# Masking half the units on ScalarE and GpSimd, a one-step leaky rectifier, 32-bit weight rests and a new static order

## The chip, the cores and the metric

The program runs on one core of a Trainium2 chip. The metric is device time in microseconds (us) from launch to the end of one execution. Engines: PE is the matrix engine (PEld its weight loads), DVE the vector engine, ACT the scalar engine, POOL the GpSimd engine, and SP the queue that issues the transfers (DMA).

## The reference

Attention with a top-32 mask on 4 batches of 8 heads, 576 positions and 64 dimensions, then two feed-forward layers on the 2304 tokens:

```
scores = q @ k^T / 8
kth    = the 32nd largest score of each row
scores = where(scores >= kth, scores, -1e9)
attn   = exp(scores - max); attn = attn / (sum(attn) + 1e-9)
x      = attn @ v, heads side by side               # 2304 x 512
h = x @ w1_in;  g = max(0.01 * h, h);               x = g @ w1_out    # 512 -> 2048 -> 512
h = x @ w2_in;  g = s * max(h, 0)^2 + b;          out = g @ w2_out
```

The weights arrive as float64 bits; nothing is converted on the host.

## The kernel before, in words

All products are made in float16 halves: a number is scaled by a power of two and split into a high and a low float16, and a product takes three matrix products (high x high, high x low, low x high).

**Units and tiles.** The 2304 tokens make 18 tiles of 128 rows (two of the 18 are made of the last 64 rows of two batches). A unit is one tile and one pair of heads, so there are 72 units, four to a tile. A unit runs: `qk` on PE (scores into PSUM), `s_ev` on ACT (copy to the tile `s`), on DVE for each head four rounds of `max` (the eight largest, `mx`) with three `match_replace` (`wk`) between them, which leave the 32nd largest score in the last place of `mx`; `expo` on ACT (`em`); `mask` on DVE, which multiplies the exponentials by (score >= 32nd) and sums them (`L811`); then the halves `e_hi` on ACT and `e_lo` on POOL, a transposing transfer `e_turn` into `ahl`, `pv_mm` on PE, and `x_ev` on DVE (`L904`), which writes the unit's columns of the tile's row block `x`. The first `EB` units (7) make their halves and the transpose on PE instead of `e_lo` and `e_turn`.

**Weights.** Each of the four matrices (1i, 1o, 2i, 2o) has 16 blocks of 512 KB. A block is loaded (`w_load`), DVE moves exponent and fraction into place (`w_shift`, `L343`), ACT rounds the rest of the fraction (`w_rest`, `L348`), DVE keeps sign and top exponent bit (`w_sign`, `L353`), POOL adds the two as integers (`w_round`, `L357`). Four blocks share a scale, from a norm that PE makes (`w_norm`). The halves are then made in one of the ways that `WM` names: P by PE and ACT, D with a DVE step (`lo_d`, `L454`), G with a DVE step (`pre`) and a POOL step. 1i and 1o stay on the chip; the halves of 2i and 2o go to memory (`w_out`). `finals1` (`L541`) ends the preparation of layer one, `finals` (`L558` to `L570`) that of layer two.

**Feed-forward.** Tiles are taken in blocks, one tile at a time for the first ten and two at a time for the other eight. Each layer: `m_in` (`L1022`, 12 products for each of 16 weight blocks, 128 or 256 columns), the rectifier in groups of 128x512 (`a1` to `a5`), `m_out` (`L1093`, 3 products of 512 columns for each tile and weight block). In layer one the leaky rectifier is `a1` = relu on ACT, `a2` = a second, negated and scaled relu on ACT (`L1054`), `a3` = their difference on POOL (`L1058`). The weights of layer two are streamed from memory for each block of tiles by 512 KB loads (`st_i`, `st_o`); two of the 16 pairs stay on the chip.

**The order.** A planner (`Plan`) writes the order of every engine's instructions before the program is built: each engine takes, when it is free in the plan, the ready step with the lowest key. Keys come from `W0`, `WD` (weights), `KO` (offsets of loads and first units) and the unit's number; the durations in the `add` calls, `HOP` (from one engine to the next) and the buffers of each ring (`BUFS`) decide when a step is ready. On the chip each engine then runs its list in that order and waits where an operand isn't there. The rings `em` and `ahl` have one buffer, `s` has four, `raw` three.

## Time and profile before

| what | us |
|---|---|
| three executions | 1250.7, 1255.13, 1255.96 (median 1255.13) |
| the profiled execution, first to last instruction (span) | 1250.3 |
| busy: PE / DVE / ACT / POOL | 1070.3 / 1036.9 / 827.4 / 842.1 |
| layer one's scales ready (`L541`) | 186.15 |
| 12th, 13th and 72nd `x_ev` | 310.17, 320.11, 1098.27 |
| last PE instruction to the end | 1246 to 1250.3 |

The profile gives no device time of its own for the profiled execution; its span lies 0.4 us under the fastest of the three. Busy time of PE is modelled at its ends: successive products overlap by a little, so the starts in the timeline are the better measure of what a group costs (start to start). On DVE a `max` shows 0.744 us but the next instruction starts 0.66 us after it.

### The profile page before, as it was taken

What the parts mean: (1) busy time and instruction counts of PE and PEld (TensorE: products, weight loads), DVE (VectorE), ACT (ScalarE), POOL (GpSimd) and SP (SyncE); (2) the same over time, 40 slices, a digit from 0 to 9 for tenths busy, and PEclk for the clock granted to TensorE, in tenths of its full rate; (3) what the DMA queues carried; (4) which work ended last, traced back from release to release, by engine and by line L of the source; (5) the groups of instructions that cost most, each with busy time, mean ns of one, the idle gap of its engine ahead of it and who ended that gap; (6) DMA issues with size and microseconds to landing.
All of it is one profiled execution on the core that took longest, in us unless ns stands there. A gap on an engine that the chain in (4) does not pass through costs nothing.

```text
span 1250.3 us, 27997 instructions
## 1 busy us (share of the span) xinstructions
PE 1070.3 (86%) x10520; PEld 735.6 (59%) x10520; DVE 1036.9 (83%) x2437; ACT 827.4 (66%) x1427; POOL 842.1 (67%) x1126
## 2 busy tenths in 40 slices
PE   2666767788888988988998989789989799899998
PEld 1333334556666766665776666566566466666665
DVE  4999899999989999999999999889999999800000
ACT  7887998866577766667876665558876565444321
POOL 5776555657678877677887776658887666655542
PEclk9877898999999999999999999989999999999999
DMA  7767776478889898888899797988445568510444
GB/s 180 237 217 213 198 199 198 148 165 211 218 158 240 199 263 183 220 201 223 221 237 248 165 249 162 261 231 195 83 80 114 149 162 228 153 26 18 133 162 161
DMA packets 362408, 228.39 MB, mean 183 GB/s; under 512 B 276512, under 2 KB 301088, under 8 KB 362272
## 3 DMA queue, kind: packets, MB, share of 16 engines
q1 hardware_dynamic: 362272, 226.61, 71.5%
q8 instruction: 82, 1.34, 0.5%
q14 instruction: 54, 0.44, 0.1%
HBM read 151.52 MB, written 13.11 MB: 132 GB/s over the span
## 4 chain that ended last, share of the span: by engine, by line
DVE 24%; PE 22%; DMA 17%; POOL 9%; issue 4%; ACT 4%; SPq 1%; DVEq 0%; POOLq 0%; ACTq 0%
DMA ahl<-ehl 10%; DVE mx L786 9%; PE acc L1093 9%; PE h L1022 9%; DVE wk L795 8%; DVE em L811 5%; POOL ehl L869 3%; DMA st_o<-sc_2o 2%; PE pv L897 2%; POOL g L1070 2%; DMA qn<-in_q_dram 1%; POOL r L1058 1%; PE sc L768 1%; DMA vn<-in_v_dram 1%; DMA st_i<-sc_2i 1%
## 5 line engine op out<-in xcount | busy, mean ns | idle before, releaser
L786 DVE MAX8 mx<-wk 128x8 f32<-128x576 f32 x432 | 311.3, 744 | 0.0
L1093 PEld LDWEIGHTS <-g 128*128 128x128 f16 x1728 | 159.5, 98 | 141.0 <-issue 23.7
L1022 PE MATMUL h<-early,wreg 128*128 128x128 f16 (+1 forms) x2688 | 224.2, 235 | 5.1 <-DMA early<-xhl 3.5
L1022 PEld LDWEIGHTS <-wreg 128*128 128x128 f16 x2688 | 194.3, 98 | 52.8 <-issue 5.1
L1093 PE MATMUL acc<-wreg,g 128*128 128x512 f16 x864 | 222.8, 380 | 0.2 <-DVE o L1152 0.2
L795 DVE MATCH_REPLACE8 wk<-mx,wk 128x576 f32<-128x576 f32 x288 | 212.7, 741 | 0.0
L1093 PE MATMUL acc<-st_o,g 128*128 128x512 f16 x756 | 194.5, 379 | 12.9 <-DMA st_o<-sc_2o 12.6
L869 POOL TENSOR_TENSOR ehl<-em,ehl 128x576 f16<-128x576 f32 x130 | 168.0, 1298 | 50.1 <-ACT ehl L865 49.7
L1022 PE MATMUL h<-xT,st_i 128*128 128x128 f16 (+1 forms) x2352 | 198.5, 236 | 2.3 <-DMA st_i<-sc_2i 2.0
L1022 PEld LDWEIGHTS <-st_i 128*128 128x128 f16 x2352 | 170.3, 99 | 45.5 <-DMA st_i<-sc_2i 5.0
L1050 ACT ACTIVATE r<-h,cg 128x512 f32<-128x512 f32 x144 | 98.3, 683 | 93.7 <-PE h L1022 74.8
L811 DVE SCALAR_TENSOR_TENSOR em<-s,mx,em 128x576 f32<-128x576 f32 x144 | 155.0, 1087 | 0.3 <-ACT em L808 0.2
L865 ACT CAST ehl<-em 128x576 f16<-128x576 f32 x130 | 86.4, 668 | 93.0 <-DVE em L811 67.1
L808 ACT ACTIVATE em<-s,st,est 128x576 f32<-128x576 f32 x144 | 121.8, 861 | 18.9 <-POOL st L789 14.9
L1067 ACT ACTIVATE g<-r 128x512 f16<-128x512 f32 x144 | 89.9, 626 | 64.1 <-PE acc L1093 44.5
L897 PE MATMUL pv<-vhl,ahl 128*128 128x64 f16 (+3 forms) x2160 | 86.6, 201 | 49.8 <-DMA ahl<-ehl 47.6
L897 PEld LDWEIGHTS <-ahl 128*128 128x128 f16 (+1 forms) x2160 | 79.6, 104 | 71.9 <-DMA ahl<-ehl 66.8
L1058 POOL TENSOR_TENSOR r<-r,early 128x512 f32<-128x512 f32 x72 | 93.6, 1300 | 38.2 <-ACT early L1054 37.9
L1062 POOL TENSOR_TENSOR early<-r 128x512 f32<-128x512 f32 x72 | 75.7, 1052 | 62.1 <-ACT r L1050 61.4
L774 ACT COPY s<-sc 128x576 f32<-128x576 f32 x144 | 91.5, 636 | 35.0 <-PE sc L768 31.8
L768 PE MATMUL sc<-kT,qT 128*128 128x288 f16 (+1 forms) x640 | 99.2, 297 | 11.2 <-ACT s L774 9.7
L786 DVE MAX8 mx<-s 128x8 f32<-128x576 f32 x144 | 107.0, 746 | 0.3 <-ACT s L774 0.3
(191 smaller groups left out, 1741.0 us busy)
## 6 DMA issues: line engine op xcount, KB each, us to landing
st_i<-sc_2i SPq DMA_DIRECT2D x98, 512.0 KB, 4.8
st_o<-sc_2o SPq DMA_DIRECT2D x98, 512.0 KB, 4.8
raw_2i<-in_moe_w_in_dram SPq DMA_DIRECT2D x16, 512.0 KB, 4.9
wreg<-in_moe_w_in_dram SPq DMA_DIRECT2D x16, 512.0 KB, 5.7
raw_1o<-in_moe_w_out_dram SPq DMA_DIRECT2D x16, 512.0 KB, 4.0
raw_2o<-in_moe_w_out_dram SPq DMA_DIRECT2D x16, 512.0 KB, 4.1
qn<-in_q_dram SPq DMA_DIRECT2D x16, 256.0 KB, 4.8
sc_2i<-hl_2i SPq DMA_DIRECT2D x16, 256.0 KB, 2.4
```

What stands on the lines that cost most here:

```text
L768: nc.tensor.matmul(pt[a, c, 0:288], lhsT=qT[u][:, h, z, a], rhs=kT[b, p][:, 576 * h + 288 * c:576 * h + 288 * c + 288], start=(z == 0), st ...
L774: nc.scalar.copy(sc[u, h], box["pt"][:, :, 0:288])
L786: nc.vector.max(out=mx[u][:, h, r, :], in_=wk[u, h] if r else flat(sc[u, h]))
L795: nc.vector.match_replace(out=wk[u, h], in_to_replace=mx[u][:, h, r, :], in_values=src, imm_value=NEG)
L808: nc.scalar.activation(em[u][:, h, :], flat(sc[u, h]), AF.Exp, bias=st[u][:, h:h + 1], scale=est[:, 0, u:u + 1])
L811: nc.vector.scalar_tensor_tensor(em[u][:, h, :], flat(sc[u, h]), mx[u][:, h, 3, 7:8], em[u][:, h, :], op0=ALU.is_ge, op1=ALU.mult, accum_o ...
L869: nc.gpsimd.tensor_tensor(ehl[u][:, 1, a], em[u][:, h, :], ehl[u][:, 0, a], op=ALU.subtract)
L897: nc.tensor.matmul(pt[a, o0:o1], lhsT=ahl[u][:, za, blk * P + a.start:blk * P + a.stop], rhs=vt[:, zv, v0:v1], start=(i == 0 and za == 0 a ...
L1022: nc.tensor.matmul(box["h"][:, n * T:(n + 1) * T], lhsT=w[:, ew, c, :], rhs=src[:, ex, c, :], start=(c == 0 and ew == 0 and ex == 0), stop ...
L1050: nc.scalar.activation(box["r1"], box["h"], AF.Relu, scale=cg[:, 2 * l, 3, gi:gi + 1])
L1058: nc.gpsimd.tensor_tensor(box["r1"], box["r1"], box["r2"], op=ALU.subtract)
L1093: nc.tensor.matmul(accs[i, l, tt], lhsT=ghl[i, l, g][:, eg, n * T + tt * P:n * T + (tt + 1) * P], rhs=w[:, ew], start=(f == 0 and eg == 0 ...
```

## The change

- **The mask of three units in eight** (`MK`, letters A; 27 of 72 units): POOL multiplies the 32nd largest score by 2^98 (`t_big`); ACT writes relu(2^98 x 32nd - 2^98 x score), which is zero where the score is kept and huge where it isn't (`above`); POOL subtracts that from the score (`less`); ACT takes the exponential and sums it (`expo2`). The DVE mask falls away there. The other 45 units are as before.
- **The leaky rectifier** of layer one is one ACT step (`AF.Prelu`, slope 0.01); `a2` and the POOL difference are gone.
- **The rest of the weights** is written as a 32-bit integer; `w_sign` reads the raw word and the shifted word, keeps the upper two bits of the first and joins them (two tensors, 32 bits, instead of one, 16 bits), and no longer waits for `w_rest`.
- **Smaller ones:** P-made weight halves 56 instead of 48 blocks, `lo_d` and `pre` 4 each instead of 8; norms of four blocks in one go; ten instead of seven units turned by PE; `raw` two buffers instead of three.
- **The order** is written with other durations, a model of transfers by kind (`XFER`), steps of DVE and POOL that hold each other up in the plan (`lock`), rings that are taken in the order of the code (`IN_LINE`), other keys, the matrices in the order 1i, 1o, 2o, 2i, and all 18 tiles one at a time (`BLOCKS`).

```diff
-BUFS = {... "raw": 3, ...}
-WM = {"1i": "PPP", "1o": "P", "2i": "PG", "2o": "DP"}
-ORDER = ("1i", "1o", "2i", "2o")
+BUFS = {... "raw": 2, ...}
+WM = {"1i": "PPPP", "1o": "PPPP", "2i": "GPPP", "2o": "PPDP"}
+ORDER = ("1i", "1o", "2o", "2i")
+IN_LINE = ("mx", "em", "ehl", "ahl", "x32", "s", "wk", "kT", "vT", "qT", ...)
+MK = "DADDAADD"
-EB = 7
+EB = 10
-W0 = {"1i": -14.81, "1o": -9.79, "2i": -14.83, "2o": -0.65}
+W0 = {"1i": -39.03, "1o": -3.45, "2i": -32.04, "2o": -4.3}
-NB = 10
+BLOCKS = [1, 1, 1, 1, 1, 1, 1, 1, 1, 1, 1, 1, 1, 1, 1, 1, 1, 1]
...
         def w_rest(m=m, f=f):
-            nc.scalar.activation(t[:, :, 0], t[:, :, 1], AF.Copy, scale=2.0 ** -13)
+            nc.scalar.activation(raw[m, f].rearrange("p (n t) -> p n t", t=2)[:, :, 0], t[:, :, 1], AF.Copy, scale=2.0 ** -13)
         def w_sign(m=m, f=f):
-            nc.vector.tensor_scalar(t[:, :, 1], t[:, :, 3], 0xC000, None, op0=ALU.bitwise_and)
+            d = wT[m, f].bitcast(I32)
+            nc.vector.scalar_tensor_tensor(d, raw[m, f].rearrange("p (n t) -> p n t", t=2)[:, :, 1], -(1 << 30), d,
+                                           op0=ALU.bitwise_and, op1=ALU.bitwise_or)
...
+            def t_big(u=u):
+                nc.gpsimd.tensor_tensor(st[u][:, 8:10], mx[u][:, :, 3, 7], big.to_broadcast([P, 2]), op=ALU.mult)
+            def above(u=u, h=h):
+                nc.scalar.activation(em[u][:, h, :], flat(sc[u, h]), AF.Relu, bias=st[u][:, 8 + h:9 + h], scale=-BIG)
+            def less(u=u, h=h):
+                nc.gpsimd.tensor_tensor(em[u][:, h, :], flat(sc[u, h]), em[u][:, h, :], op=ALU.subtract)
+            def expo2(u=u, h=h):
+                nc.scalar.activation(em[u][:, h, :], em[u][:, h, :], AF.Exp, bias=st[u][:, h:h + 1], scale=est[:, 0, u:u + 1],
+                                     accum_out=st[u][:, 2 + h:3 + h])
+            if MK[u % len(MK)] == "D":
...
+            else:
+                if h == 0:
+                    x_big = add(POOL, 0.15, t_big, mxd, key + 0.7, use=[tm])
+                x = add(ACT, 0.6, above, [x_big] + ([x_exp] if h else []), ...)
+                x = add(POOL, 1.37, less, [x], ...)
+                mk.append(add(ACT, 0.8, expo2, [x, ex[h]], ...))
...
             def a1(g=g, box=box):
-                nc.scalar.activation(box["r1"], box["h"], AF.Relu, scale=cg[:, 2 * l, 3, gi:gi + 1])
-            def a2(g=g, box=box):
-                nc.scalar.activation(box["r2"], box["h"], AF.Relu, scale=cg[:, 1, 3, g * nf // 4:g * nf // 4 + 1])
                 if l == 0:
-                    nc.gpsimd.tensor_tensor(box["r1"], box["r1"], box["r2"], op=ALU.subtract)
+                    nc.scalar.activation(box["r1"], box["h"], AF.Prelu, scale=cg[:, 0, 3, gi:gi + 1], alpha=0.01)
```

What the planner makes of it is seen in the lists of the engines. First DVE, where it comes to layer one's scales (`finals1`; `cg` are the scales, `mx` and `wk` the rounds of a unit, `T_2o` and `raw_2o` a weight block). Before, from row 305 of 1847:

```order
L353 TENSOR_SCALAR raw_2o_1648<-raw_2o_1648 128x512
L303 TENSOR_SCALAR cg<-cg 128x1
L343 TENSOR_SCALAR T_2o_1725<-raw_2o_1663 128x512
L413 TENSOR_SCALAR cI_1o_1729<-ident,cg 128x128
L534 TENSOR_REDUCE consts<-cg 128x1
L541 SCALAR_TENSOR_TENSOR cg<-cg 128x4
```

After, from row 197 of 1777:

```order
L371 TENSOR_SCALAR T_2o_1273<-raw_2o_1230 128x512
L331 TENSOR_SCALAR cg<-cg 128x1
L829 MATCH_REPLACE wk_1_1228<-mx_1151,wk_1_1228 128x576
L381 SCALAR_TENSOR_TENSOR T_2o_1273<-raw_2o_1230,T_2o_1273 128x512
L442 TENSOR_SCALAR cI_1o_1280<-ident,cg 128x128
L569 TENSOR_REDUCE consts<-cg 128x1
L576 SCALAR_TENSOR_TENSOR cg<-cg 128x4
```

Ahead of `finals1` stood 49 `max`, 10 masks, 50 shifts and 49 sign steps; now 28 `max`, 4 masks, 34 shifts and 34 sign steps. At the 12th `x_ev` there stood 104 `max`, 25 masks, 8 `lo_d`, 8 `pre`; now 106, 16, 4 and 4.

Second PE, behind the last attention product (`h` is what `m_in` writes, `acc` what `m_out` writes). Before, the last rows of it and the first of each kind behind it:

```order
L897 MATMUL pv_16270<-vhl_94,ahl_16233 128x64
L1093 LDWEIGHTS g_0_1_16168
L1093 MATMUL acc_0_1_16206<-wreg,g_0_1_16168 128x512
L1022 LDWEIGHTS wreg
L1022 MATMUL h_0_6_16251<-early,wreg 128x256
```

After:

```order
L956 MATMUL pv_17932<-vhl_96,ahl_17876 128x64
L1081 LDWEIGHTS wreg
L1081 MATMUL h_0_2_17881<-early,wreg 128x128
L1151 LDWEIGHTS g_0_1_17822
L1151 MATMUL acc_0_0_17809<-wreg,g_0_1_17822 128x512
```

Behind the last attention product stood 51 `m_in` steps of 256 columns (19 of layer one, 32 of layer two) and 123 `m_out` steps; now 69 `m_in` steps of 128 columns (21 and 48) and 73 `m_out` steps. Between the 12th and the end of the 72nd attention product stood 272 `m_in` steps of 128 and 77 of 256 columns, 413 `m_out` and 130 `qk` steps; now 459 of 128 columns, 463 `m_out` and 129 `qk`.

Third ACT, where it masks an A unit now (`em` is the unit's tile, `ahl` and `etp` another unit's halves). After:

```order
L903 CAST ahl_2821<-etp_8_2848 128x128
L855 ACTIVATE em_2851<-s_0_2619,st_2650 128x576
L910 CAST ahl_2821<-etp_8_2848 128x128
L855 ACTIVATE em_2851<-s_1_2696,st_2650 128x576
L861 ACTIVATE em_2851,st_2650<-em_2851,st_2650,est 128x576
L808 COPY s_0_2881<-sc_0_2871 128x576
```

The two `above` steps stand close together ahead of the first exponential, which waits for POOL's first `less`; the next unit's score copy stands behind it. ACT's list holds one table load before and one now.

## Rows read from the trace of the kernel before

**Rows 1.** Page, parts 1 and 2: busy us of each engine, busy tenths.

```profile
PE 1070.3 (86%) x10520; PEld 735.6 (59%) x10520; DVE 1036.9 (83%) x2437; ACT 827.4 (66%) x1427; POOL 842.1 (67%) x1126
DVE  4999899999989999999999999889999999800000
```

**Rows 2.** Windows: stretch, its us, busy us (instructions) per engine, clock, DMA share, GB/s.

```profile
0.00:186.00 186.00, 113.69 (x575) 60.23 (x575) 161.20 (x373) 158.32 (x252) 117.18 (x158) 0.88 0.74 208
186.00:310.00 124.00, 102.34 (x1082) 69.75 (x1080) 121.47 (x283) 94.45 (x161) 79.12 (x96) 0.96 0.68 175
310.00:798.00 488.00, 436.06 (x5346) 319.70 (x5342) 464.66 (x1109) 336.56 (x604) 365.90 (x520) 0.99 0.89 214
310.00:1098.00 788.00, 706.88 (x7887) 509.82 (x7884) 745.68 (x1752) 524.06 (x931) 577.41 (x812) 0.99 0.80 194
1098.00:1250.00 152.00, 147.34 (x989) 95.83 (x985) 8.58 (x31) 50.61 (x86) 68.36 (x60) 1.00 0.32 99
```

**Rows 3.** Timeline, DVE: start, us; scales ready, 12th, 13th, 49th, 72nd `x_ev`.

```profile
186.15 0.16 DVE L541 SCALAR_TENSOR_TENSOR cg<-cg 128x4 f32<-128x4 f32 x1
310.17 0.28 DVE L904 TENSOR_TENSOR x<-pv,st 128x128 f32<-128x128 f32 x1
320.11 0.28 DVE L904 TENSOR_TENSOR x<-pv,st 128x128 f32<-128x128 f32 x1
799.28 0.29 DVE L904 TENSOR_TENSOR x<-pv,st 128x128 f32<-128x128 f32 x1 [2.77 <-PE pv L897]
1098.27 0.29 DVE L904 TENSOR_TENSOR x<-pv,st 128x128 f32<-128x128 f32 x1 [8.18 <-PE pv L897]
```

**Rows 4.** Timeline, PE: start to start gives what each kind of step costs.

```profile
605.02 0.65 PE L768 MATMUL sc<-kT,qT 128*128 128x288 f16 x4
605.51 0.83 PE L1022 MATMUL h<-xT,st_i 128*128 128x128 f16 x12
606.18 0.81 PE L1093 MATMUL acc<-kept_o,g 128*128 128x512 f16 x3
...
1097.20 1.03 PE L897 MATMUL pv<-vhl,ahl 128*128 128x128 f16 x27
1098.07 0.81 PE L1093 MATMUL acc<-wreg,g 128*128 128x512 f16 x3
1098.72 1.47 PE L1022 MATMUL h<-early,wreg 128*128 128x256 f16 x12
1100.03 0.81 PE L1093 MATMUL acc<-wreg,g 128*128 128x512 f16 x3
```

**Rows 5.** Groups by line: busy us, mean ns of one, idle us before it.

```profile
L811 DVE SCALAR_TENSOR_TENSOR em<-s,mx,em 128x576 f32<-128x576 f32 x144 | 155.0, 1087 | 0.3 <-ACT em L808 0.2
L353 DVE TENSOR_SCALAR raw_1o<-raw_1o 128x512 uint16<-128x512 uint16 x16 | 14.2, 891 | 3.1 <-ACT raw_1o L348 2.9
L454 DVE SCALAR_TENSOR_TENSOR hl_2o<-T_2o,cg,hl_2o 128x512 f16<-128x512 f32 x8 | 9.0, 1129 | 0.0
L448 DVE TENSOR_SCALAR T_2i<-T_2i,cg 128x512 f32<-128x512 f32 x8 | 5.6, 724 | 0.0
L348 ACT ACTIVATE raw_1o<-raw_1o 128x512 uint16<-128x512 uint16 x16 | 21.9, 1390 | 0.0
L1054 ACT ACTIVATE early<-h,cg 128x512 f32<-128x512 f32 x72 | 49.2, 683 | 1.1 <-POOL g L1070 1.1
L808 ACT ACTIVATE em<-s,st,est 128x576 f32<-128x576 f32 x144 | 121.8, 861 | 18.9 <-POOL st L789 14.9 <-POOL ehl L869 3.7
L1058 POOL TENSOR_TENSOR r<-r,early 128x512 f32<-128x512 f32 x72 | 93.6, 1300 | 38.2 <-ACT early L1054 37.9 <-POOL vhl L666 0.2
```

**Rows 6.** Two DVE lines with two inputs: ns of one, min/median/max.

```profile
L811 DVE SCALAR_TENSOR_TENSOR em<-s,mx,em x144: 775/873/1901, 35.1 to 1086.7; 128x576 f32<-128x576 f32 x144
L454 DVE SCALAR_TENSOR_TENSOR hl_2o<-T_2o,cg,hl_2o x8: 719/914/1812, 200.3 to 249.0; 128x512 f16<-128x512 f32 x8
```

**Rows 7.** DMA view, 310 to 798 us: all that was moved.

```profile
DMA packets 182481, 104.41 MB, mean 214 GB/s; under 512 B 147591, under 2 KB 151687, under 8 KB 182414
```

More of the change, by code (lines that the diff above doesn't have):

```diff
@@ L99, in order @@
         remain = [t[1] for t in self.by_tok]
+        line = {r: iter(self.rings[r].line) for r in IN_LINE}
+        turn = {r: next(line[r], None) for r in IN_LINE}
         last = [0.0] * len(remain)
         start, self.end, moved = [None] * N, [0.0] * N, 0.0
-        events = []
+        events, held = [], {"DVE": 0.0, "POOL": 0.0}
         for n in range(N):
@@ L134, in order @@
                     for k in self.take[n]:
-                        self.rings[self.by_tok[k][0]].live.append(k)
+                        r = self.rings[self.by_tok[k][0]]
+                        r.live.append(k)
+                        if self.by_tok[k][0] in turn:
+                            turn[self.by_tok[k][0]] = next(line[self.by_tok[k][0]], None)
+                            for e_, it in r.wait:
+                                heapq.heappush(events, (now, it[1], "ready"))
+                            r.wait = []
                     start[n] = now
@@ L269 @@
     nc.vector.memset(neg1, -1.0)
+    big = one.tile([P, 1], F32, name="big")
+    nc.vector.memset(big, BIG)
     tiny = one.tile([P, 2], F32, name="tiny")
@@ L881 @@
                 lo.append((x, y))
[L882 removed]
+            x = add(SP, XFER["e_turn"], e_turn, [y for _, y in lo], ke, take=[ta], use=[th])
             lo = [(x, x)]
@@ L918 @@
     blocks, t = [], 0
-    for n in [1] * NB + [2] * ((NTL - NB) // 2):
+    for n in BLOCKS:
         blocks.append(list(range(t, t + n)))
@@ L1075, in layer @@
                 x = add(ACT, 0.571, a1, [x, fin1], ka, take=[t1], use=[th])
-                x = add(ACT, 0.571, a2, [x], ka, take=[t2], use=[th])
-                x = y = add(POOL, 1.225, a3, [x], ka, use=[t1, t2])
                 x = add(ACT, 0.52, a4, [x], ka, take=[tg], use=[t1])
```

202 lines of the change are left out of this document (113 added, 89 removed).

## Prediction

> **What bounds the kernel now.** I read the page first, then the same engines by stage, then the places where the stages meet. The page shows two engines that are both nearly full, PE at 86% and DVE at 83% of the span [rows 1]. But the row of tenths shows that DVE is at nine almost everywhere up to slice 35 and at zero behind it: DVE sets the pace of the first 1098 us, PE alone that of the last 152 [rows 1, 3]. The windows make three stages of it [rows 2]. In the first, up to 186 us, the weights are prepared: DVE is busy for 161 and ACT for 158 of 186 us, PE for only 114, since layer one cannot start before its scales are there (186.15 us, rows 3). From the 12th `x_ev` (310 us) to the 72nd (1098 us) DVE is busy for 745.7 of 788 us, which is 94.6%, PE for 707, POOL for 577, ACT for 524. Behind that PE is busy for 147 of 152 us and DVE for 9.
>
> So there are three clocks to follow: when the early work is done, how fast a unit goes by in the middle, and how much of the feed-forward work is left for PE behind the last unit.
>
> **Prices.** On PE start to start is the price [rows 4]: `qk` 0.49 us, `m_in` of 128 columns 0.67, of 256 columns 1.31, `m_out` 0.65, `pv_mm` 0.87. A tile taken alone therefore costs PE as much as in a pair (2 x 0.67 against 1.31); what it costs more is DMA, since each block of tiles streams layer two's weights again.
>
> **The early stage.** DVE is the engine to count. Up to the 12th `x_ev` nine masks go (25 to 16, 1.087 us each, -9.8), four `lo_d` (1.129, -4.5) and four `pre` (0.724, -2.9), and two `max` and one `match_replace` come (about +2) [rows 5]. The sign step is new: two tensors of 32 bits in place of one of 16, 64 times. No row shows it; the nearest is `lo_d`, also two 128x512 tensors in and one out, with 0.719 us at best, 0.914 in the middle and 1.129 in the mean, against 0.891 of the old step [rows 5, 6]. The bounds are 64 x (0.719 - 0.891) = -11 us and 64 x (1.129 - 0.891) = +15; I take the middle value, +1.5. Sum: -14, say 15 us, because the sign step also stops waiting for `w_rest` (the 3.1 us of the one matrix shown). The 13th `x_ev` moves from 320 to 305 us. The scales of layer one move further: 21 `max`, 6 masks, 16 shifts and 15 sign steps that stood ahead of them now stand behind, so PE gets feed-forward work some 45 to 55 us earlier. I give that no term of its own; it only means that PE is not behind when the middle begins.
>
> The mask shows 775 ns at best and 1901 at worst, `lo_d` 719 and 1812 [rows 6]. The Trainium skill (GPSIMD Engine Reference, Specifications) says that GpSimd shares its SBUF interfaces with the vector engine, against instructions with two SBUF inputs among others; the spread of both lines agrees with that. By that rule the new sign step, with its two inputs, is as exposed as `lo_d`, which would put it at the mean and the early sum at 15 - 13.7 = about 1 us instead of 15.
>
> `w_rest` costs ACT 1.390 us now; with 32-bit output it lies between that and 0.683, the price of a 512-element ACT step with 32-bit output [rows 5]. That is 0 to 45 us of ACT, which is not the engine I count, so it is worth nothing by itself; if it stays at 1.39, ACT at 158 of 186 us is no worse off than before, as 16 blocks less stand ahead of the scales.
>
> **The middle.** DVE: from the 12th to the 72nd `x_ev` 119 masks become 74, 45 x 1.087 = -49 us, so its 745.7 us become 697 [rows 2, 5]. ACT: `above` and the exponential's sum come in 23 units, 46 steps of about 0.86 at most (+40, priced by the exponential), and 60 `a2` of 0.683 go (-41): nothing. POOL: 46 `less` at 1.300 come (+60), 60 differences at 1.300 go (-78): about -18 of 577 [rows 2, 5]. Neither becomes a bound. What A units do add is a longer way from the last `max` to the halves: `t_big`, `above`, `less`, `expo2` across two engines, about 0.2 + 0.7 + 1.3 + 0.9 = 3.1 us and four hand-overs in place of one mask of 1.1. Behind `above` on ACT stand the next unit's score copy and the rectifier; behind `less` on POOL the next unit's small steps; the single `em` and `ahl` buffers mean that the next unit's exponential waits for them.
>
> PE: the change of `BLOCKS` and of the keys puts feed-forward work into this stage that stood behind it. From behind the 12th to the end of the 72nd attention product, before: 272 x 0.67 + 77 x 1.31 + 413 x 0.65 + 130 x 0.49 + 60 x 0.87 = 667 us. After: 459 x 0.67 + 463 x 0.65 + 129 x 0.49 + 60 x 0.87 = 724 us [rows 4]. It was 667 of the 778 us from the 13th to the 72nd `x_ev`; now PE has 724, more than DVE's 697, and becomes the engine that sets the pace.
>
> DMA: from 310 to 798 us, where tiles go one by one, its engines are busy for 0.89 of the time, 434 us for the 37 units between the 12th and the 49th `x_ev`, 11.7 us and 104.4/37 = 2.82 MB for a unit [rows 2, 3, 7]. All units now go like that. For 59 units this is 692 us.
>
> So 724 (PE), 697 (DVE) and 692 (DMA) lie within 5% of each other. None can be filled wholly, because each engine runs a fixed list and waits for the others. Before, the engine that bound filled 94.6%. I take the same for PE: 724/0.946 = 765 us in place of 778.
>
> **The end.** Behind the last attention product stood 51 x 1.31 + 123 x 0.65 = 147 us of PE work; the trace shows 152 us from the last `x_ev` to the end [rows 2, 3, 4], so some 5 us for waits and the last store. Now it is 69 x 0.67 + 73 x 0.65 = 94 us. Layer two of three tiles lies in these 94 us, one alone at the end, with fewer other steps to fill a wait; I add 8 us: 102, which is 50 us less.
>
> **The sum.** 305 + 765 + 102 = 1172 us of span, against 320 + 778 + 152 = 1250. The profiled execution is given by its span alone, 1250.3, which is 4.8 us under the median of the three runs (and 0.4 under the fastest); I add these 4.8: **1177 us**, 6% less than 1255.13.
>
> **Rivals.**
>
> *PE runs through (0.14).* At the end of the kernel PE fills 147 of about 148 us when nothing holds it. If the new order feeds it as well in the middle, that takes 730 us: 305 + 730 + 102 + 4.8 = 1142. For it: layer one starts earlier, so there is always feed-forward work at hand. Against it: PE, DVE and DMA are too close together.
>
> *The middle gains nothing (0.19).* The longer way of the A units with one `em` buffer eats what DVE gave up, or the early stage stays where it is. Then the middle takes 778 us (1190) or up to 13.8 us for a unit, 815 us (1227). For it: PE's waits for `ahl` and DVE's 8 us wait ahead of the last `x_ev` [rows 3] show that the attention chain is already late at times. Still faster, since the end is shorter in any case.
>
> *DMA binds, and it gets slower (0.08).* 59 units of 2.82 MB are 166 MB. From 310 to 1098 us the queues moved 194 GB/s in the mean [rows 2]; if that were all that a full middle gets, it would take 858 us, and 305 + 858 + 102 + 4.8 = 1270. It decides from below 198 GB/s, where the middle passes 843 us. For it: share 0.89 already, most packets under 512 B [rows 7]. Against: 214 GB/s at that share, which leaves 240 at a full one. The Trainium skill (DMA: Bandwidth & Descriptors, Specifications) gives about 358 GB/s as the limit of one core's memory; by that there would be no such case. The trace doesn't agree that this is the limit that counts here, as 0.89 is reached at 214.
>
> **How the numbers follow.** 0.59 for the forecast, whose own range is 1151 to 1199 (PE filled to 98% or 92% in the middle: 739 or 787 us), 0.14, 0.19 and 0.08 for the rivals. The range from 1143 to 1222 takes in nearly all of the first two and most of the third. About 0.5%, 6 us, is what can be told from no change. All but the DMA case are faster; it splits into 0.06 slower and 0.02 about equal, and I leave 0.01 of the others for about equal and 0.01 for slower: faster 0.90, same 0.03, slower 0.07.
>
> **What would show it.** Right: 90 masks on DVE; layer one's scales before 140 us; the 13th `x_ev` near 305; about 12.9 us for a unit behind that; PE busy near 95% in the middle, and about 100 us from the last `x_ev` to the end. The sign step near 0.9 us, `w_rest` nearer 0.7. Wrong: DMA share near 1 with waits for `st_i` and `st_o` over 30 us on PE (the DMA case); DVE idle for more than 80 us in the middle with waits on ACT's exponential or POOL's `less` (the chain); or scales still at 186 us.

## The result, and the profile after

The changed kernel takes 1268.97 us (median of 4 runs, 1266.42 to 1274.95) against 1252.91 us before, timed beside it on the same chip: a ratio of 1.0129, 95% interval [1.0095, 1.0164]. It is slower by 1.3%, where 1177 us and 6% less had been forecast. The profiled span is 1268.7 us where the sum said 1172, so 97 us are to be found.

The page of the changed kernel, parts 1 and 2, answers to [rows 1]: busy us of each engine, then busy tenths of DVE.

```profile
PE 1092.3 (86%) x12116; PEld 771.0 (61%) x12116; DVE 970.7 (77%) x2321; ACT 801.5 (63%) x1483; POOL 803.6 (63%) x1125
DVE  4649888897999679898887898888669999993100
```

DVE gave up 66 us, as meant, but it no longer has a nine in nearly every slice: it waits, in the early stage and in the middle. The windows of the changed kernel, cut where the forecast cut them (13th and 72nd `x_ev`), answer to [rows 2]; columns as there.

```profile
0.00:354.50 354.50, 246.64 (x1809) 150.01 (x1810) 278.53 (x671) 241.83 (x470) 201.61 (x270) 0.85 0.64 184
354.50:1166.00 811.50, 750.85 (x9266) 553.62 (x9264) 684.82 (x1633) 531.03 (x966) 565.33 (x822) 0.99 0.86 208
1166.00:1268.70 102.70, 94.82 (x1047) 67.39 (x1044) 7.31 (x18) 28.68 (x48) 36.62 (x33) 1.00 0.67 214
```

Stage by stage, forecast against measured: early 305 and 354.5 (+49.5), middle 765 and 811.5 (+46.5), end 102 and 102.7 (+0.7). The end is right; the two losses are nearly equal in size and, as the runs below show for most of them, different in kind.

The groups by line of the changed kernel answer to [rows 5]: mask, sign step (two of its four groups), rest, and the two new steps of an A unit.

```profile
L845 DVE SCALAR_TENSOR_TENSOR em<-s,mx,em 128x576 f32<-128x576 f32 x90 | 83.6, 940 | 7.8 <-ACT em L842 7.8
L381 DVE SCALAR_TENSOR_TENSOR T_1o<-raw_1o,T_1o 128x512 int32<-128x512 int32 x16 | 12.5, 797 | 0.0
L381 DVE SCALAR_TENSOR_TENSOR T_2o<-raw_2o,T_2o 128x512 int32<-128x512 int32 x16 | 11.2, 698 | 0.0
L376 ACT ACTIVATE raw_1o<-raw_1o 128x512 int32<-128x512 uint16 x16 | 10.9, 684 | 3.3 <-DMA raw_1o<-in_moe_w_out_dram 3.2
L855 ACT ACTIVATE em<-s,st 128x576 f32<-128x576 f32 x54 | 40.4, 769 | 22.7 <-POOL st L849 22.4
L858 POOL TENSOR_TENSOR em<-s,em 128x576 f32<-128x576 f32 x54 | 77.2, 1443 | 16.0 <-ACT em L855 13.2 <-PE sc L802 2.8
```

The prices were not the fault. The sign step came out below the forecast (0.70 to 0.80 us for 0.91), the rest at its lower end (0.68), `above` below (0.77 for 0.86); only `less` is dearer (1.44 for 1.30).

**The middle, by who waits for whom.** Four groups of the changed kernel, 354.5 to 1166 us; the number behind the bar's second half is the idle time before them and what ended it.

```profile
L1151 PE MATMUL acc<-st_o,g 128*128 128x512 f16 x588 | 159.6, 382 | 12.3 <-DMA st_o<-sc_2o 11.0 <-ACT vj L676 1.2
L956 PE MATMUL pv<-vhl,ahl 128*128 128x64 f16 (+2 forms) x1809 | 69.8, 198 | 38.7 <-DMA ahl<-ehl 38.3 <-DVE wk L829 0.2
L963 DVE TENSOR_TENSOR x<-pv,st 128x128 f32<-128x128 f32 x59 | 16.9, 287 | 59.4 <-PE pv L956 59.0
L820 DVE MAX8 mx<-s 128x8 f32<-128x576 f32 x114 | 85.6, 750 | 17.5 <-ACT s L808 17.5
```

PE waits for the turned exponentials (`ahl`, a transfer) and for streamed weights. DVE waits most for PE's attention product (59.0 us), and for 17.5 us for ACT's copies of the scores. DVE idles for 127 of 811 us, which the prediction had named as the sign of the A units' chain, but the releasers are mostly others: for an exponential of ACT it waits 6.3 us, for POOL's denominators 15.6 us, and 13.5 us of these last remain in the run below that has every mask on DVE. The queue that issues all transfers, SP, waits too (what it waited for: us in total, times, longest); L1060 loads layer two's weights for the stream.

```profile
SPq L1060 <- PE h L1081: 93.5, 49, 9.8
SPq L1060 <- PE acc L1151: 61.4, 36, 4.1
```

Such a load waits until PE has done with the buffer that it will fill, and every turn of exponentials behind it in the queue waits with it. The two lines make 155 us; in the middle of the kernel before they were 75.5 and 47.7, 123 us. At the turns themselves SP waits still longer, for POOL's halves: 196 us over all of POOL's steps. But that was 214 us before, so it is not what the change added.

**The early stage.** SP's timeline of the kernel before, then of the changed one (start, us): first turns and loads of weights.

```profile
10.27 1.35 SPq L738 DMA_TRANSPOSE qT<-qhl  x1
11.67 0.57 SPq L334 DMA_DIRECT2D raw_2i<-in_moe_w_in_dram  x1
12.47 1.31 SPq L617 DMA_TRANSPOSE kT<-khl  x1
```

```profile
2.14 3.68 SPq L362 DMA_DIRECT2D wreg<-in_moe_w_in_dram  x4
...
17.79 1.35 SPq L772 DMA_TRANSPOSE qT<-qhl  x1
...
23.72 4.15 SPq L651 DMA_TRANSPOSE kT<-khl  x1
```

The new keys put four loads of weights ahead of the first unit's keys, and ten ahead of the first turn of keys (`kT`), where one stood before. The first unit's scores come later, and its first `max` later still. ACT's copy of these scores and that `max`, before and then after:

```profile
19.91 0.62 ACT L774 COPY s<-sc 128x576 f32<-128x576 f32 x1
20.76 0.75 DVE L786 MAX8 mx<-s 128x8 f32<-128x576 f32 x1
```

```profile
35.05 0.66 ACT L808 COPY s<-sc 128x576 f32<-128x576 f32 x1
50.26 0.74 DVE L820 MAX8 mx<-s 128x8 f32<-128x576 f32 x1
```

Before, the `max` starts 0.2 us after its scores are there; now it starts 14.5 us after, behind shifts and sign steps of weights that stand ahead of it in DVE's list. The first `x_ev` starts at 106 us (51 before). Windows of the first 100 us, before and then after, show what DVE does meanwhile (its busy time is the third, behind PE's and PEld's).

```profile
0.00:50.00 50.00, 19.55 (x107) 12.74 (x107) 31.98 (x82) 40.01 (x74) 30.24 (x55) 1.00 0.78 205
50.00:100.00 50.00, 34.03 (x158) 17.34 (x159) 46.95 (x101) 39.93 (x56) 35.88 (x39) 0.76 0.74 229
```

```profile
0.00:50.00 50.00, 15.66 (x54) 8.48 (x55) 25.66 (x58) 33.25 (x68) 33.45 (x49) 0.87 0.95 272
50.00:100.00 50.00, 34.54 (x131) 17.91 (x130) 28.84 (x84) 32.12 (x63) 31.16 (x48) 0.69 0.42 110
```

DVE works for 54.5 of 100 us where it worked for 78.9. First the transfers are full (0.95), and then they are more than half idle (0.42). Up to the first `x_ev` DVE idles for 46 us (18 before), from there to the 13th for 30 (10 before): 48 us more in all, which is the loss of this stage. Of the 46 us it waits 11.0 for loads of weights, 8.8 for ACT's sums of squares of the queries, 8.6 for PE's norms of the keys, and the rest in small parts for further steps of other engines. PE's granted clock is 0.85 of full speed in the mean of this stage (0.91 before); what that costs no run tells.

### The profile page after: what moved, and what is told of

Its sections match the earlier page's. It is cut to its first block, busy times and chain, and to the rows that moved or that the text cites. A ratio compares the mean times of both kernels' runs of the same rounds, so it can differ in the third digit from the quotient of the medians.

```text
span 1268.7 us, 31192 instructions
## 1 busy us (share of the span) xinstructions
PE 1092.3 (86%) x12116; PEld 771.0 (61%) x12116; DVE 970.7 (77%) x2321; ACT 801.5 (63%) x1483; POOL 803.6 (63%) x1125
## 4 chain that ended last, share of the span: by engine, by line
PE 42%; DMA 32%; DVE 9%; ACT 7%; POOL 4%; issue 3%; SPq 2%; POOLq 0%; ACTq 0%; DVEq 0%
PE h L1081 16%; DMA ahl<-ehl 16%; PE acc L1151 15%; DMA st_o<-sc_2o 4%; PE pv L956 4%; DVE mx L820 3%; PE sc L802 3%; DMA st_i<-sc_2i 3%; DMA qT<-qhl 2%; DVE wk L829 2%; DMA qn<-in_q_dram 2%; DMA raw_2i<-in_moe_w_in_dram 1%; PE wlo_1i L491 1%; POOL ehl L928 1%; DMA wreg<-in_moe_w_in_dram 1%
## 5 line engine op out<-in xcount | busy, mean ns | idle before, releaser
L1081 PEld LDWEIGHTS <-wreg 128*128 128x128 f16 x3456 | 215.4, 99 | 54.0 <-issue 3.2
L1081 PE MATMUL h<-early,wreg 128*128 128x128 f16 x3456 | 236.6, 220 | 0.7 <-DMA early<-xhl 0.5
L1151 PE MATMUL acc<-wreg,g 128*128 128x512 f16 x864 | 235.5, 382 | 0.0
L1081 PEld LDWEIGHTS <-st_i 128*128 128x128 f16 x3024 | 183.4, 98 | 42.8 <-DMA st_i<-sc_2i 7.6
L1081 PE MATMUL h<-xT,st_i 128*128 128x128 f16 x3024 | 200.9, 219 | 5.5 <-DMA st_i<-sc_2i 5.5
L928 POOL TENSOR_TENSOR ehl<-em,ehl 128x576 f16<-128x576 f32 x124 | 157.7, 1283 | 50.8 <-ACT ehl L924 49.0
L1129 POOL TENSOR_TENSOR g<-r,g 128x512 f16<-128x512 f32 x72 | 84.6, 1175 | 76.3 <-ACT g L1126 76.0
L820 DVE MAX8 mx<-s 128x8 f32<-128x576 f32 x144 | 107.9, 750 | 17.5 <-ACT s L808 17.5
L829 DVE MATCH_REPLACE8 wk<-mx,s 128x576 f32<-128x576 f32 x144 | 106.8, 742 | 0.0
L1113 ACT ACTIVATE r<-h,cg 128x512 f32<-128x512 f32 x72 | 49.3, 684 | 69.5 <-PE h L1081 69.1
L845 DVE SCALAR_TENSOR_TENSOR em<-s,mx,em 128x576 f32<-128x576 f32 x90 | 83.6, 940 | 7.8 <-ACT em L842 7.8
```

The source lines that it names most:

```text
L820: nc.vector.max(out=mx[u][:, h, r, :], in_=wk[u, h] if r else flat(sc[u, h]))
L829: nc.vector.match_replace(out=wk[u, h], in_to_replace=mx[u][:, h, r, :], in_values=src, imm_value=NEG)
L845: nc.vector.scalar_tensor_tensor(em[u][:, h, :], flat(sc[u, h]), mx[u][:, h, 3, 7:8], em[u][:, h, :], op0=ALU.is_ge, op1=ALU.mult, accum_o ...
L928: nc.gpsimd.tensor_tensor(ehl[u][:, 1, a], em[u][:, h, :], ehl[u][:, 0, a], op=ALU.subtract)
L1081: nc.tensor.matmul(box["h"][:, n * T:(n + 1) * T], lhsT=w[:, ew, c, :], rhs=src[:, ex, c, :], start=(c == 0 and ew == 0 and ex == 0), stop ...
L1129: nc.gpsimd.tensor_tensor(ghl[i, l, g][:, 1], box["v"], ghl[i, l, g][:, 0], op=ALU.subtract)
```

## The experiments

Fifteen further kernels were run. Letters of theories belong to the expectation that they stand in. "New order" is the changed kernel's, "old order" that of the kernel before; a kernel "in its own order" has the same instructions in the same places, with more buffers or less data. The three stages are given as early + middle + end, from one profiled execution each.

**A third buffer for the weights' bits.** The change cut these from three to two. The first run gives the buffer back without planning anew, the second plans with it.

```diff
+REAL = {"raw": 3}
-        return pl.tile(shape, dtype, tag=name, name=label, bufs=BUFS[name])
+        return pl.tile(shape, dtype, tag=name, name=label, bufs=REAL.get(name, BUFS[name]))
```

> The changed kernel with its order of instructions unchanged, but a third buffer for the raw weight blocks (the plan still counts two). Theory A, the early stage is held by the two raw buffers (48 blocks come in between 57 and 269 us, about 4.0 us each for 2o and 2i, though load, rest, shift, sign and round of one block follow each other in about 7.8 us): loads are issued earlier, the blocks of 2o and 2i come every 3 us or less, layer two's scales come before 280 us instead of 297, and the time falls by 10 to 20 us. Rival, the static lists of DVE, ACT and POOL hold the pace and the loads only fit them: scales within 5 us of 297, time within 5 us of 1269.

> The changed kernel with three raw buffers in the plan too, so the order is written anew with the same keys. Theory A: layer two's scales near 260 us, 13th x_ev near 320 instead of 354, time 1235 to 1250. Rival, the keys (weights first, attention late) make the early stage slow: scales earlier by less than 10 us, time 1260 to 1275.

In its own order: 1268.35 us, ratio to before 1.0136 [1.0097, 1.0174]; 348.2 + 810.0 + 103.6. Planned anew: 1292.28 us, 1.032 [1.0285, 1.0355]; 355.3 + 811.7 + 124.4. The buffer is worth about 6 us of the early stage in the profiles (348 to 350 us in this execution and the two below that have it in the same order, 354 to 360 in three that do not) and nothing that the timing can tell. The second run lies outside both ranges of its expectation. Planning with the buffer brought layer one's scales to 137 us, but the 13th `x_ev` stayed and the end grew by 22 us: scales that are early are no gain by themselves, and an order made anew moves things that nobody meant to move.

**The masks and the blocks.**

```diff
-MK = "DADDAADD"
+MK = "D"
```

> The changed kernel with every unit masked by DVE as before, order written anew by the same planner and keys. Theory B, PE and its waits set the pace behind the 13th x_ev and the DVE time that the A units save (49 us there) buys nothing: time 1255 to 1285, main stage within 15 us of 812. Rival, the A units' longer chain (less 1.44 us instead of 1.30, waits of ACT and POOL) is what makes the main stage slow: main stage below 790, time below 1250. Second rival, DVE's load still counts: main stage above 835, time above 1295.

```diff
-BLOCKS = [1, 1, 1, 1, 1, 1, 1, 1, 1, 1, 1, 1, 1, 1, 1, 1, 1, 1]
+BLOCKS = [1] * 10 + [2] * 4
```

> The changed kernel with the last eight tiles taken in pairs as before, order written anew. Theory C, streaming layer two's weights for 18 blocks instead of 14 (29 MB more, DMA share 0.86 in the main stage) delays the transposes that pv waits for: main stage below 790, time 1235 to 1255 even if the end is longer. Rival, DMA is not what holds: main stage falls only by the PE work that moves to the end, and the time stays within 15 us of 1269.

All masks on DVE: 1305.21 us, 1.0419 [1.0378, 1.046]; 358.3 + 834.3 + 106.8. So the kernel with A units (27 of the 72, which is less than the half that the title says) is 36 us faster (1305.21 less 1268.97), and its middle 23 us: they are not what makes it slow. How much of the 36 us is theirs stays open, as the order was written anew for this run, and writing it anew alone cost 24 us with the third buffer. Pairs at the end: 1286.53 us, 1.0262 [1.0224, 1.03]; 354.2 + 797.4 + 135.8. The middle has 23 us less PE work (727.7 us busy) and a lower DMA share (0.78), and is only 14 us shorter. I read this as speaking against the transfers. It was a poor test: it moved work, order and bytes at once, and the run with half the bytes overturned the reading.

**Transfers in the middle of the new order.** One run gives the stream a fifth buffer in its own order (`REAL = {"wst": 5}`, as above). The other halves what each load of the stream brings:

```diff
-                        nc.sync.dma_start(out=w.rearrange("p u e n -> p u (e n)"),
-                                          in_=sc16["2" + kind][2 * j:2 * j + 2].rearrange("u p n -> p u n"))
+                        nc.sync.dma_start(out=w[:, :, 0], in_=sc16["2" + kind][2 * j:2 * j + 2, :, 0:512].rearrange("u p n -> p u n"))
...
-                            nc.tensor.matmul(box["h"][:, n * T:(n + 1) * T], lhsT=w[:, ew, c, :], rhs=src[:, ex, c, :],
+                            nc.tensor.matmul(box["h"][:, n * T:(n + 1) * T], lhsT=w[:, ew if l == 0 else 0, c, :], rhs=src[:, ex, c, :],
...
```

> The changed kernel in its own order, with a fifth buffer for the blocks of layer two's weights that are loaded again for each block of rows (98 pairs of loads in the middle stage). In the trace of the changed kernel the queue of transfers waits at these loads for TensorE (144.6 us for the first product, 87.5 us for the second, over the middle stage), and every turn of exponentials stands behind them. Theory A (the middle is lost in the queue: loads that wait for a buffer hold back the turns): the middle stage falls from 811.5 to 795-803 us, the total to about 1250-1260 us. Rival B (the middle is lost in the transfers' own time, 208 GB/s and 85% of the engines busy): the waits at the loads shrink, but the turns land no earlier; middle 808-812, total 1264-1270 us. Rival C (the order of the steps on the engines sets it): the same as B.

> The changed kernel in its own order; each load of layer two's weights in the stream brings only the high halves (256 KB in place of 512), and layer two's products of streamed weights read the high halves three times, so that all engines have the same instructions as before and its result leaves the weights' low halves out. Theory B (transfers: 38 more loads than in the kernel before, each 512 KB, make the turns of exponentials land later, and TensorE and VectorE wait for them): the middle falls from 811.5 to 770-785 us, the waits of pv for ahl from 38 us to under 25, of VectorE for pv from 59 to under 30, the total to 1215-1240 us. Rival C (the order, made with durations that do not hold, and not the bytes): the middle stays over 800 us, the total over 1255. The stage up to the 13th x_ev (354 us) stays within 4 us in both, since nothing is streamed there.

Fifth buffer: 1250.59 us, 0.9957 [0.9927, 0.9987]; 360.4 + 796.6 + 99.6 (the profiled execution was the slowest of ten, 1258.4 us). SP's waits of both kinds at these loads fall in the middle from 155 to 49 us (144.6 and 87.5 us in the expectation are those of the whole execution, not of the middle):

```profile
SPq L1061 <- PE h L1082: 36.7, 26, 4.7
SPq L1061 <- PE acc L1152: 12.3, 15, 2.6
```

PE's wait for `ahl` falls from 38.3 to 26.1 us with it, although a turn lands hardly sooner (5.6 us in the median for 5.7): what went away is the waiting in the queue.

Half the bytes: 1210.36 us, 0.9637 [0.96, 0.9675]; 355.0 + 757.0 + 99.1. Its window of the middle and three groups there:

```profile
355.00:1112.00 757.00, 737.75 (x9267) 549.71 (x9266) 684.41 (x1634) 529.96 (x967) 567.70 (x823) 1.00 0.71 155
```

```profile
L1150 PE MATMUL acc<-st_o,g 128*128 128x512 f16 x588 | 157.8, 379 | 1.8 <-DMA st_o<-sc_2o 1.8
L956 PE MATMUL pv<-vhl,ahl 128*128 128x64 f16 (+2 forms) x1809 | 69.1, 198 | 13.6 <-DMA ahl<-ehl 13.5
L963 DVE TENSOR_TENSOR x<-pv,st 128x128 f32<-128x128 f32 x60 | 16.9, 282 | 32.8 <-PE pv L956 32.5
```

With half the bytes, and not one instruction moved, the middle falls by 54 us to 757, below the 765 forecast and below the range expected here, and PE is busy for 97% of it. The number of packets stays (284,908 and 285,029). PE waits 13.5 us for the turned exponentials in place of 38.3, DVE 32.5 us for PE's product in place of 59.0. So the middle's loss is time of the transfers. The DMA views of the changed kernel and of this one say how (KB each, median us from issue to landing):

```profile
st_i<-sc_2i SPq DMA_DIRECT2D x98, 512.0 KB, 4.6
st_o<-sc_2o SPq DMA_DIRECT2D x98, 512.0 KB, 5.1
ahl<-ehl SPq DMA_TRANSPOSE x59, 5.7
```

```profile
st_i<-sc_2i SPq DMA_DIRECT2D x98, 256.0 KB, 3.2
st_o<-sc_2o SPq DMA_DIRECT2D x98, 256.0 KB, 3.4
ahl<-ehl SPq DMA_TRANSPOSE x59, 5.1
```

Both sorts land sooner, the turns too, whose own size did not change. The waits in the queue, on the other hand, stay at 152 us:

```profile
SPq L1060 <- PE h L1080: 92.8, 56, 8.2
SPq L1060 <- PE acc L1150: 59.2, 42, 3.4
```

So the two runs take away two different things: the fifth buffer the waiting of the loads in the queue (15 us of the middle), half the bytes the late landing (54 us). The table of durations that made the new order (in the diff) gives 3.6 us to a load of the stream and 4.58 to a turn of exponentials; they take 4.6 to 5.1 and 5.7. The Trainium skill (DMA: Bandwidth & Descriptors, Anatomy of one DMA) puts one transfer at about 2.0 us plus its bytes at 436 GB/s, measured on transfers that GpSimd issues; an estimate by that page is 3.2 us for 512 KB and 2.6 for 256. Here the same sizes take 1.4 to 1.9 us more at a share of 0.86, and 0.6 to 0.8 us more at 0.71. That sum holds no load on the engines; how much of the difference is the load and how much the other path, no run separates.

**The functions without the new order.** Old order, each new instruction in the place of the one it replaces. First the rectifier and the weights' rest; then also the masks, with `above` and `less` where the mask stood and the exponential at the next step that reads it. In both, two of the 64 sign steps are missing (two blocks of 2i).

```diff
-                nc.scalar.activation(box["r1"], box["h"], AF.Relu, scale=cg[:, 2 * l, 3, gi:gi + 1])
+                if l == 0:
+                    nc.scalar.activation(box["r1"], box["h"], AF.Prelu, scale=cg[:, 0, 3, gi:gi + 1], alpha=0.01)
...
-            nc.vector.tensor_scalar(t[:, :, 1], t[:, :, 3], 0xC000, None, op0=ALU.bitwise_and)
+            d = wT[m, f].bitcast(I32)
+            nc.vector.scalar_tensor_tensor(d, raw[m, f].rearrange("p (n t) -> p n t", t=2)[:, :, 1], -(1 << 30), d,
+                                           op0=ALU.bitwise_and, op1=ALU.bitwise_or)
...
```

> The kernel before in its own order, instruction for instruction, with two of the new functions put in their places: the leaky rectifier in one step (the second rectifier and GpSimd's subtraction are gone) and the weights' rest as 32-bit integers with the one-step sign. No new keys, no new planner, no mask by ACT. Theory D (the functions are good, and the new order loses it): VectorE's sign falls from 0.82-1.04 to about 0.7-0.8 us x64, ACT's rest from 1.39 to 0.68 us x64, in the stage where VectorE is 91% busy: the 13th x_ev comes at 305-315 us in place of 320; the middle keeps its 778 us, since VectorE bounds it and nothing of its work there changes (770-780); total 1230-1245 us. Rival E (the functions themselves lose: the wider reads of the sign and the rest slow down what shares a port with them): 1250-1265 us, with the 13th x_ev at 320 or later.

> As the last, and with the masks of units 1, 4 and 5 of each eight done by ACT and GpSimd: the two steps ahead of the exponential stand where the mask stood in the order, the exponential itself at the next step that needs it. Theory D: VectorE loses 44 masks of 1.09 us in the middle (736 to about 688 us busy), and TensorE (699 us busy) bounds it: the middle falls from 778 to 740-765, the total to 1195-1225 us. Rival E (GpSimd's difference of 1.43 us and the two ACT steps are longer than the mask they replace, and the turn of exponentials waits for them): the middle stays at 775-800 us, the total at 1240-1270.

Rectifier and rest: 1248.28 us, 0.9936 [0.9915, 0.9957]; 319.8 + 776.7 + 152.8. With the masks: 1326.91 us, 1.0592 [1.055, 1.0635]; 333.8 + 837.3 + 152.5. The first is a small gain, between the ranges of theories D and E; its profile does not show where the gain lies, as no stage moves by more than 2 us. The early stage does not move, though 0.7 us of each rest is gone from ACT. The sign step is no cheaper than the one it replaced there (0.89 us in [rows 5]):

```profile
L359 DVE SCALAR_TENSOR_TENSOR T_1o<-raw_1o,T_1o 128x512 int32<-128x512 int32 x16 | 14.1, 887 | 0.1
```

The second fell on the rival's side and beyond. An A unit's four steps in a list that was made for one mask hold up what stands behind them; two groups of its middle show where:

```profile
L829 ACT ACTIVATE em<-s,st 128x576 f32<-128x576 f32 x44 | 34.0, 772 | 40.6 <-POOL st L828 40.4
L830 POOL TENSOR_TENSOR em<-s,em 128x576 f32<-128x576 f32 x44 | 62.8, 1427 | 53.7 <-ACT em L829 52.4 <-PE sc L780 1.3
```

ACT stands idle for 40 us and POOL for 52 at these places. The masks need an order made for them, and in the new order they had one.

**The weights' loads in the early stage.** New order, half of the weights' bits loaded, each half read twice.

```diff
-                nc.sync.dma_start(out=t, in_=w[P * f:P * (f + 1), :])
+                nc.sync.dma_start(out=t[:, 0:512], in_=w[P * f:P * (f + 1), 0:512])
...
-            t = raw[m, f].rearrange("p (n t) -> p n t", t=2)[:, :, 1]
+            t = raw[m, f][:, 0:512].rearrange("p (n t) -> p n t", t=2)[:, :, 1].unsqueeze(1).to_broadcast([P, 2, 256])
...
```

> The changed kernel in its own order; each load of the weights' float64 bits brings 256 KB in place of 512, and the three steps that take them apart read the loaded half twice, so that every step has its old size and the weights' other half is left out. What is open is where the early stage lost its 50 us against the forecast: in its first 50 us the transfers are 95% busy (272 GB/s, 78% and 205 GB/s in the kernel before), the first x_ev comes at 106 us (51 before), and VectorE is busy for 54.5 of the first 100 us (78.9 before). Theory G (the weights' loads, put first, hold back the first units' keys and queries): the first x_ev comes at 80-95 us, the 13th at 325-342 in place of 354, total 1240-1258. Rival H (the order on the engines holds the units back, whatever the loads take): first x_ev 100-106, the 13th 347-354, total 1260-1270.

1258.47 us, 1.0005 [0.997, 1.004]; 341.8 + 804.8 + 103.6. The first `max` starts at 43.0 us in place of 50.3, the first `x_ev` at 97.7 in place of 106, the 13th 13 us sooner. The 13th `x_ev` and the total lie at the edge of theory G's ranges, the first `x_ev` between G's and H's. The halved loads gave back about a quarter of the 50 us (the profiled execution was 6.5 us faster than the median of this run). DVE's idle time shows a larger share: up to the 13th `x_ev` it is 54 us in place of 76, which is 22 of the 48 us that the change added. The run is not quite clean, as the steps that read the half twice cost DVE 9 us more (288 us busy for 278.5). DVE's own waits for the loads of `1i`, whole execution, with all bits and then with half:

```profile
DVE wreg L371 <- DMA wreg<-in_moe_w_in_dram: 11.0, 8, 2.9
DVE wreg L371 <- DMA wreg<-in_moe_w_in_dram: 0.9, 1, 0.9
```

These waits are nearly gone, and the waits for ACT's sums of squares and PE's norms stay (10.2 and 7.5 us up to the 13th `x_ev`, 11.0 and 9.5 with all bits). So what is left, 26 us, looks like the order of the steps more than the loads; a run with smaller loads still was not made.

**Whether the transfers held the kernel before as well.** The same halved stream, and the same fifth buffer (two buffers instead of three for the rows' halves, to make room), in the kernel before.

> The kernel before, functions and order, with the stream's loads of layer two halved as in the run of the changed kernel (the weights' low halves are left out). Theory (the middle of the kernel before was bound by VectorE alone, 94.6% busy): middle 765-778 us, so the change turned the transfers into a limit they had not been. Rival (the transfers held that middle back as well): middle 730-755 us, the waits of pv for ahl from 44 us to under 25.

> The kernel before, functions and order, with the fifth buffer for the stream and two in place of three for the rows' halves: nothing of the change. With the one-step rectifier and the 32-bit rest the same gave a middle of 762 us and 1236 us. Theory (all of that is the buffer, the functions are worth the 8 us that they gave alone): middle 762-768, total 1240-1246. Rival (the functions make the room that the buffer uses): middle 772-778, total 1249-1256.

Half the stream: 1230.21 us, 0.9807 [0.9769, 0.9845]; 323.0 + 754.7 + 150.6. Fifth buffer: 1246.84 us, 0.9929 [0.9901, 0.9958]; 323.9 + 769.7 + 152.8. The halved stream's middle:

```profile
323.00:1077.70 754.70, 693.73 (x7794) 501.48 (x7792) 737.24 (x1727) 515.99 (x916) 570.70 (x804) 0.99 0.65 143
```

DVE is busy for 98% of it; PE's wait for `ahl` is 32 us (44 with all bytes), not under 25:

```profile
L897 PE MATMUL pv<-vhl,ahl 128*128 128x64 f16 (+2 forms) x1809 | 69.8, 198 | 35.2 <-DMA ahl<-ehl 32.4 <-DVE em L811 1.3 <-DVE wk L795 1.0
```

So transfers held the old middle as well: half of the stream's bytes are worth 23 us there and 54 in the new one. With half of them the two middles are the same length (755 and 757), the new one with 44 us more PE work in it (57 were reckoned), and the end is 51 us shorter. The fifth buffer takes SP's waits at the loads from 123 to 16 us and gives 8 us of the middle; the run lies between its two theories, nearer the first. Set side by side, half stream against half stream, the changed kernel is 1210.36 to 1230.21 us: there, by the medians, the change is faster by 1.6% (the two were timed beside kernels before of 1256.39 and 1257.02 us). What is left against it is the early stage, 355 to 323 us.

**Versions that beat both.** New order with both buffers; the same with a third pair of weights kept on the chip (13 loads a block, not 14, and two buffers for the rows' halves); new keys, chosen on a reckoning with landing times of the traces; and the old order with rectifier, rest (all 64 sign steps on their own blocks), fifth buffer and, to make room, two buffers for the rows' halves.

```diff
+REAL = {'wst': 5, 'raw': 3}
...
-MK = "DADDAADD"
-EB = 10
+MK = "DADADADD"
+EB = 18
```

(The first line is the first version; the third has it too, and other values in `W0`, `WD`, `KO` and `WM`.)

> The changed kernel in its own order with both further buffers: a third for the weights' bits in the early stage, a fifth for the stream of layer two. If the two gains are of different stages they add: the early stage 348 us (as with the third buffer alone), the middle 797 (as with the fifth alone), total 1240-1248 us. If the early gain is taken back by the middle, 1250 us as with the fifth alone.

> As the last, and one more pair of layer two's weights stays on the chip after its first load (13 loads for each block of rows in place of 14; the buffers of the rows' halves go from three to two to make room). Theory B (the transfers set the middle): half the streamed bytes gave 54 us in the middle, so a fourteenth of them gives about 8 us: middle 785-792, total 1230-1242 us. Rival C (only the queue's waiting for buffers mattered, and the fifth buffer has taken that away): middle 795-800, total 1240-1250.

> The changed kernel's steps and both further buffers, in another order: keys chosen with the landing times that the traces show (loads of the stream 4.8 us, turns of exponentials 5.6, other turns 4.5) in place of 3.6, 4.58 and 3.15. Theory F (the order lost because it was made with transfers that land too soon): middle 775-790, total 1222-1240 us. Rival (an order made anew loses as much elsewhere as it gains, as with the third buffer planned in: 1292 us): total 1250-1290.

> The kernel before in its own order with the one-step rectifier, the 32-bit rest and a fifth buffer for the stream (two in place of three for the rows' halves, to make room). If the loads that wait for a buffer hold back the turns there too: middle 777 to 765-770 us, total 1230-1240. If VectorE, 94% busy there, is all that counts in the middle of the old order: middle 774-778, total 1244-1250.

| kernel | us | ratio to before, 95% | early + middle + end |
|---|---|---|---|
| new order, both buffers | 1243.68 | 0.991 [0.9877, 0.9943] | 348.0 + 793.8 + 100.0 |
| third pair kept | 1244.89 | 0.9916 [0.9884, 0.9947] | 350.0 + 795.6 + 98.9 |
| new keys | 1240.39 | 0.9857 [0.9826, 0.9887] | 350.5 + 778.9 + 109.3 |
| old order, fifth buffer | 1235.96 | 0.9836 [0.9805, 0.9868] | 320.0 + 762.1 + 152.0 |

In the stages the gains of the two buffers stand side by side (348.0 early, 793.8 middle); by the timing, both together and the fifth alone are not told apart. The third pair gave nothing where 8 us were expected; that is what the rival said, for whom only the queue's waiting for buffers mattered. The run moved 162 MB in its middle where the first moved 169. It changed two things (a pair kept, a buffer of the rows' halves given up), and whether one took back what the other gave stays open; but bytes saved are not simply time saved. The new keys shorten the middle by 15 us and lengthen the end by 9; against the first row the intervals overlap. The last is the fastest of those that leave nothing out: the kernel before, its order untouched, with one more buffer, one rectifier less and a narrower rest. By themselves functions and buffer gave 0.64% and 0.71%, together 1.64%.

## Why the prediction was wrong

**The end: right.** 102.7 us for 102. PE work counted step by step and a few us for waits held.

**The prices: right or on the safe side**, as shown above. The sum of DVE's work held as well: 278.5 us up to the 13th `x_ev` where 292 less 15 was reckoned, 684.8 in the middle for 697.

**The early stage: the step that failed is "The 13th `x_ev` moves from 320 to 305 us".** It let the milestone fall with DVE's sum and so took DVE's idle time, 28 us before, as given. It became 76 us. The order put the weights first; I had read that as earlier scales for layer one, which came (151 us; I said before 140), and gave it no cost. Its cost is that the first unit has nothing on DVE until 50 us. Shown: functions alone in the old order leave the stage at 320; halved loads give back 13 us (22 us of DVE's idle time), the third buffer 6. Some 20 to 30 us remain. For these the trace names waits for steps of ACT and PE in their new places, and shows 14.5 us in which the first scores are ready while DVE's list has weights first. That they are the order of the steps is read from the trace; no run isolated it.

**The middle: the step that failed is "692 (DMA) lie within 5% of each other. None can be filled wholly, ... I take the same for PE".** The size of the DMA term was good: a share of 0.86 over 811.5 us is 698 us. Its use was not. I compared it with PE's and DVE's sums as a third bound that would count only if it were the largest. Transfers at that share land later, each load and each turn, and one queue issues them all in a fixed list, so a load that waits for its buffer holds the next turn. PE filled 724 (the reckoned work) of 811.5 us, 89% in place of 94.6. The 94.6% had been put down to the fixed lists; with half the stream's bytes, in the same lists, DVE is busy for 98% of the old middle and PE for 97% of the new one, so most of what was missing was the transfers. Nor is the gain of 13 us there once the transfers are lightened in both: 757 us against 755. The term was also counted one unit too long: 724 us are PE's work on 60 units, from behind the 12th, and were put into the stretch of 59 from the 13th on (which made the forecast some 10 us longer, not shorter). The rival in which DMA binds looked at throughput (below 198 GB/s) and would have been refuted here, at 208 GB/s. Its total of 1270 us is the measured time within about 1 us, but by luck: it is made of 305 and 858 us for stages that took 354.5 and 811.5. The rival in which the middle gains nothing had the time nearly right (13.8 us for a unit; it is 13.75) with the wrong mechanism: DVE's waits for ACT's exponential are 6.3 us in the middle, and with all masks on DVE, in an order made anew, the kernel is 36 us slower.

The row that should have spoken was there. In [rows 3] DVE waits 8.18 and 2.77 us for PE's attention product; I used it, and "PE's waits for `ahl`" beside it, for the A units' chain, without a number for the second. Followed one step further back, to PE's product, it names the transfer; this group of the kernel before, 320 to 1098 us, was in reach:

```profile
L897 PE MATMUL pv<-vhl,ahl 128*128 128x64 f16 (+2 forms) x1807 | 70.4, 199 | 45.6 <-DMA ahl<-ehl 44.3 <-DVE mx L786 1.2
```

PE waited 44.3 us for the turned exponentials before anything was added to the queue.

**The last term, 4.8 us,** is from the span of one execution to the median of others. In every run listed the time is only 1.7 to 2.1 us over its own span; the rest was that the profiled execution was faster than that median.

## What to carry to other kernels

- Transfers at a share of 0.8 of their engines' time are not one more bound to be compared with the others; here they were a delay for everything in the queue. Before adding bytes, halve them in a run that moves no instruction: what the stage gives back is what half of them cost.
- Where one queue issues both loads that wait for buffers and transfers that an engine waits for, one more buffer for the loads can be worth more than the work removed elsewhere (15 us here, for one line).
- A forecast from busy sums assumes that the idle time stays. When the order is made anew, look at what each engine does in the first tens of microseconds of the new list before assuming it.

## What the runs showed that was not expected

The same sign step costs 0.70 to 0.80 us in the mean in the new order and 0.82 to 0.98 in the old one; the shortest take 0.66 to 0.68 us in both, and the means differ by how many take longer. What differs is what runs beside it. The Trainium skill (GPSIMD Engine Reference, Specifications) says that GpSimd shares its SBUF interfaces with VectorE and contends with vector instructions that have two SBUF inputs. That would fit, but no run here took POOL's work away to show it.

A turn of exponentials lands 0.6 us sooner (5.7 to 5.1 us) when other transfers, of which none was moved or dropped, carry half the bytes. In the kernel before the fifth buffer alone did as much (5.3 to 4.7 us), with all bytes and the same DMA share of 0.80: when the loads beside a turn start counts too, and not their bytes alone.
